# A block of adaLN, sliding-window attention and token MLP: four token groups in a pipeline instead of three stages one after another

## The chip, the cores and the metric

The kernel runs on one core of a Trainium2 chip. The metric is the device time of one execution in microseconds. A core has five engines that run their own instruction streams and wait for each other by semaphores: TensorE (PE, with its weight loads shown as PEld), VectorE (DVE), ScalarE (ACT), GpSimd (POOL) and SyncE (SP), which here issues DMAs. Matmul results land in PSUM, everything else lives in SBUF.

## The reference

x is 2048 tokens of width 512; there are 32 heads of width 16, a window of 256 tokens, and a token MLP whose hidden size is 1792.

```python
mod = (silu(c) @ w_mod).reshape(1, 6, 1, -1)          # sa, ca, ga, sb, cb, gb
h = layernorm(x) * (1 + ca) + sa
x = x + ga * attention(h, wqkv, wo)
h = layernorm(x) * (1 + cb) + sb
x = x + gb * token_mlp(h, w1, b1, w2, b2)

def attention(x, wqkv, wo):                            # H = 32, Dh = 16, W = 256
    q, k, v = split(x @ wqkv)
    scores = q @ k.T * Dh ** -0.5
    mask = (i - j >= 0) & (i - j < W)
    return softmax(where(mask, scores, -1e9)) @ v @ wo

def token_mlp(x, w1, b1, w2, b2):                      # mixes tokens, not channels
    u = gelu(einsum('bsd,sf->bdf', layernorm(x), w1) + b1)
    return (einsum('bdf,fs->bds', u, w2) + b2).transpose(0, 2, 1)
```

## The kernel before

The tokens are 16 blocks of 128 (`tb`, `kb`). The work stands in three stages. A planner orders the instructions of each engine by priority and readiness, so program order is only a hint.

**Stage 1 (lines 182 to 253).** For four groups of four blocks: LN1 on DVE with the square root on ACT (L192 to L202), transposes on PE (L207), scale and shift on ACT into `h1T` (L211), V for the group (L221, evacuated by ACT at L226 or DVE at L231), and Q and K of the first eight heads (L161, L168). K is written twice, once with the odd heads' rows set to zero and once with the even ones' (L172 to L177), so that scores can contract over 32 rows. The modulation vectors come from `w_mod` by small matmuls (L124) and broadcast ones (L245). Pool writes the constant part of the V tile, 16 memsets of 128x512 (L148), and the identity and masks.

**Stage 2, attention (L305 to L374).** Eight passes `hs` of four heads (one of two parities of a set of eight heads), each over 16 key blocks `kb`: 128 steps. A step multiplies one key block with the up to three query blocks that see it: scores (L289, contraction over 32 rows, up to 12 matmuls of 128 columns for four heads in two PSUM tiles `pss`), two exponentials of up to 768 columns on ACT (L317), the mask on DVE, which multiplies the diagonal and the far block in place (L329, L334), and PV (L347): for each head up to three matmuls with 32 stationary columns, 16 of V and 16 of ones, so that the row sums come with the product. Every fourth step DVE evacuates, transposes and divides (L357 to L374). The projections of the later heads are drawn in every fourth step up to step 44 (`pending_proj`, L255 and L324).

**Stage 3.** For each block (L424 to L473): Wo and the residual (L429, L433), LN2, modulation, the MLP's own LN, into `hb`, while the first six of 14 columns of B1 collect (L398). Then the other eight in pairs (L499) with GELU built from ACT and DVE steps (L405 to L420), and y = w2 x GELU (L519) in four groups of four blocks, each followed by two DVE steps and a store (L526 to L532). w1 and w2 are read when attention is over.

Of the kernel before, what the change touches and what calls it, by code (L numbers as in the profile page):

```python
# [8 lines left out]
DT = mybir.dt  # L9
ACT = mybir.ActivationFunctionType  # L10
ALU = mybir.AluOpType

# [5 lines left out]
WIN = 256  # L18
# [3 lines left out]
NF = F // P  # L22
EPS = 1e-5
SCORE_SCALE = DH ** -0.5
GELU_C0 = 0.044715
GELU_C1 = 1.5957691216057308


@with_exitstack
def kernel(  # L30
# [15 lines left out]
    assert tuple(A_x.shape) == (1, S, D)  # L46
    assert tuple(A_wqkv.shape) == (D, 3 * D)
    assert tuple(A_wo.shape) == (D, D)
    assert tuple(B_w1.shape) == (S, F)
    assert tuple(B_w2.shape) == (F, S)  # L50
    assert tuple(c.shape) == (1, D)
    assert tuple(w_mod.shape) == (D, 6 * D)

    x_dram = A_x[0]
    out_dram = out[0]
    dma = nc.sync

    const = ctx.enter_context(tc.tile_pool(name="const", bufs=1))
    small = ctx.enter_context(tc.tile_pool(name="small", bufs=4))
    xpool = tc.alloc_tile_pool(name="xpool", bufs=1)  # L60
    xres = [xpool.tile([P, D], DT.bfloat16, name=f"x{t}") for t in range(NT)]
# [7 lines left out]
    ident_v = identity[:].rearrange("p (a two d) -> p a two d", two=2, d=DH)  # L69
    mask_even = const.tile([P, 1], DT.float32, name="mask_even")  # L70
    nc.vector.tensor_reduce(
        out=mask_even[:], in_=ident_v[:, :, 0, :], axis=mybir.AxisListType.XY, op=ALU.add,
    )
    mask_odd = const.tile([P, 1], DT.float32, name="mask_odd")
    nc.vector.tensor_reduce(
        out=mask_odd[:], in_=ident_v[:, :, 1, :], axis=mybir.AxisListType.XY, op=ALU.add,
    )

    modFM = const.tile([P, 8], DT.float32, name="modFM")
    bc_ga = const.tile([P, D], DT.bfloat16, name="bc_ga")  # L80
    bc_cb1 = const.tile([P, D], DT.bfloat16, name="bc_cb1")
    bc_sb = const.tile([P, D], DT.bfloat16, name="bc_sb")
    bc_gb = const.tile([P, D], DT.bfloat16, name="bc_gb")
# [3 lines left out]
    modw = tc.alloc_tile_pool(name="modw", bufs=1, side="right")  # L87
    with tc.tile_pool(name="modps", bufs=2, space=bass.MemoryType.PSUM) as modps:
        wmod = modw.tile([P, ND, 6 * D], DT.bfloat16, name="wmod")
        w_mod_v = w_mod.rearrange("(j p) n -> p j n", p=P)  # L90
        c4 = modw.tile([ND, P], DT.bfloat16, name="c4")
        dma.dma_start(out=c4[:], in_=c.rearrange("o (j p) -> (o j) p", p=P))
        for t in range(4):
            dma.dma_start(out=xres[t][:], in_=x_dram[t * P : (t + 1) * P, :])
        for v in (0, 1):
            dma.dma_start(out=wmod[:, :, v * D : (v + 1) * D], in_=w_mod_v[:, :, v * D : (v + 1) * D])
        for t in range(4, 8):
            dma.dma_start(out=xres[t][:], in_=x_dram[t * P : (t + 1) * P, :])
        wqkv = const.tile([P, ND, 3 * D], DT.bfloat16, name="wqkv")
        wqkv_v = A_wqkv.rearrange("(j p) n -> p j n", p=P)  # L100
        for j in range(ND):
            dma.dma_start(out=wqkv[:, j, :], in_=wqkv_v[:, j, :])
        for t in range(8, NT):
            dma.dma_start(out=xres[t][:], in_=x_dram[t * P : (t + 1) * P, :])
        for v in (2, 4, 3, 5):
            dma.dma_start(out=wmod[:, :, v * D : (v + 1) * D], in_=w_mod_v[:, :, v * D : (v + 1) * D])

        sig4 = modw.tile([ND, P], DT.float32, name="sig4")
        nc.scalar.activation(out=sig4[:], in_=c4[:], func=ACT.Sigmoid)
        silu4 = modw.tile([ND, P], DT.bfloat16, name="silu4")  # L110
        nc.vector.tensor_tensor(out=silu4[:], in0=c4[:], in1=sig4[:], op=ALU.mult)
        st_ps = modps.tile([P, ND], DT.bfloat16, name="st_ps")
        nc.tensor.transpose(st_ps[:], silu4[:], identity[0:ND, 0:ND])
        sT = modw.tile([P, ND], DT.bfloat16, name="sT")
        nc.vector.tensor_copy(out=sT[:], in_=st_ps[:])
        sT_rep = modw.tile([P, ND, P], DT.bfloat16, name="sT_rep")
        nc.vector.tensor_copy(out=sT_rep[:], in_=sT[:].unsqueeze(2).to_broadcast([P, ND, P]))

        ps_fm = modps.tile([P, 8], DT.float32, name="ps_fm")
        for v in range(2):  # L120
            for oc in range(ND):
                col = v * ND + oc
                for k in range(ND):
                    nc.tensor.matmul(  # L124
                        ps_fm[:, col : col + 1],
                        lhsT=wmod[:, k, v * D + oc * P : v * D + (oc + 1) * P],
                        rhs=sT[:, k : k + 1],
                        start=(k == 0), stop=(k == ND - 1),
                    )
        nc.vector.tensor_copy(out=modFM[:, 0:4], in_=ps_fm[:, 0:4])  # L130
        nc.vector.tensor_scalar_add(out=modFM[:, 4:8], in0=ps_fm[:, 4:8], scalar1=1.0)

        b1b = modw.tile([P, NF], DT.bfloat16, name="b1b")
        dma.dma_start(out=b1b[:], in_=B_b1.rearrange("(j p) -> p j", p=P))
        nc.vector.tensor_copy(out=b1FM[:], in_=b1b[:])
        b2b = modw.tile([P, NT], DT.bfloat16, name="b2b")
        dma.dma_start(out=b2b[:], in_=B_b2.rearrange("(j p) -> p j", p=P))
        nc.vector.tensor_copy(out=b2FM[:], in_=b2b[:])

    otpool = tc.alloc_tile_pool(name="otpool", bufs=1)  # L140
    OTd = [otpool.tile([P, S], DT.bfloat16, name=f"OTd{g}") for g in range(ND)]
    kvpool = tc.alloc_tile_pool(name="kvpool", bufs=1)
    QT = [kvpool.tile([P, S], DT.bfloat16, name=f"QT{g}") for g in range(ND)]
    KeT = [kvpool.tile([P, S], DT.bfloat16, name=f"KeT{g}") for g in range(ND)]
    KoT = [kvpool.tile([P, S], DT.bfloat16, name=f"KoT{g}") for g in range(ND)]
    VaugT = kvpool.tile([P, NT, H, 2 * DH], DT.bfloat16, name="VaugT")
    for t in range(NT):
        nc.gpsimd.memset(VaugT[:, t, :, DH : 2 * DH], 1.0)  # L148

    def vaug_lhsT(t, head):  # L150
        return VaugT[:, t, head, :]

    pj = tc.alloc_tile_pool(name="pj", bufs=1)
    h1T = pj.tile([P, ND, S], DT.bfloat16, name="h1T")
    ps_big = tc.alloc_tile_pool(name="ps_big", bufs=2, space=bass.MemoryType.PSUM, side="right")

    def emit_qk_proj(g8, tg, evac_act):
        tok = slice(tg * 4 * P, (tg + 1) * 4 * P)
        pq = ps_big.tile([P, 4 * P], DT.float32, name="psb")
        for dc in range(ND):  # L160
            nc.tensor.matmul(  # L161
                pq[:], lhsT=wqkv[:, dc, g8 * P : (g8 + 1) * P], rhs=h1T[:, dc, tok],
                start=(dc == 0), stop=(dc == ND - 1),
            )
# [398 lines left out]
```

## Time and profile before

| | us |
|---|---|
| median of 3 runs | 411.39 (407.42 to 419.1) |
| span of the profiled execution | 404.0 |
| busy in it: PE, DVE, ACT, POOL | 350.6, 279.5, 267.8, 8.7 |

The span runs from the first to the last instruction; the launch around it is in the runs' times and not in the span. A row of the slices gives 40 equal parts of the span, each digit the busy share in tenths; PEclk is the clock that TensorE was granted, in tenths of full speed. A matmul's end is modelled and matmuls overlap, so a busy PE need not be PE at its limit: the distance from one start to the next says more than a duration.

### The profile page before, as it was taken

What the parts mean: (1) busy time and instruction counts of PE and PEld (TensorE: products, weight loads), DVE (VectorE), ACT (ScalarE), POOL (GpSimd) and SP (SyncE); (2) the same over time, 40 slices, a digit from 0 to 9 for tenths busy, and PEclk for the clock granted to TensorE, in tenths of its full rate; (3) what the DMA queues carried; (4) which work ended last, traced back from release to release, by engine and by line L of the source; (5) the groups of instructions that cost most, each with busy time, mean ns of one, the idle gap of its engine ahead of it and who ended that gap; (6) DMA issues with size and microseconds to landing.
All of it is one profiled execution on the core that took longest, in us unless ns stands there. A gap on an engine that the chain in (4) does not pass through costs nothing.

```text
span 404.0 us, 8898 instructions
## 1 busy us (share of the span) xinstructions
PE 350.6 (87%) x3713; PEld 168.9 (42%) x3713; DVE 279.5 (69%) x656; ACT 267.8 (66%) x426; POOL 8.7 (2%) x24
## 2 busy tenths in 40 slices
PE   0898997999998898988889988998996799899993
PEld 0543443444444444544444444533342344344441
DVE  6795676688978587757687666679996597522344
ACT  3486588788988888978788878859997554300000
POOL 8000000000000000000000000000000000000000
PEclk9999999699999655555555555569999999999997
DMA  7970000000000000000000000007900592001111
GB/s 221 357 152 0 2 2 2 2 2 2 2 2 2 3 2 2 2 2 2 2 2 2 2 2 2 2 2 287 408 34 0 205 412 112 0 6 48 53 54 53
DMA packets 17169, 24.70 MB, mean 61 GB/s; under 512 B 5096, under 2 KB 12776, under 8 KB 17128
## 3 DMA queue, kind: packets, MB, share of 16 engines
q1 hardware_dynamic: 17128, 24.13, 17.0%
q8 instruction: 29, 0.48, 0.5%
q14 instruction: 12, 0.10, 0.1%
HBM read 22.03 MB, written 2.10 MB: 60 GB/s over the span
## 4 chain that ended last, share of the span: by engine, by line
PE 55%; DVE 21%; ACT 18%; issue 5%; DMA 1%; SPq 0%; ACTq 0%; DVEq 0%
PE pss L289 13%; PE psb L347 13%; ACT et L317 12%; PE py L519 12%; PE pu L499 7%; PE psb L161 3%; DVE ln_stats L455 2%; PE psb L168 2%; DVE ln_stats L436 2%; PE psb L221 2%; DVE et L329 2%; ACT h1T L211 2%; DVE ln_stats L192 1%; PE psb L429 1%; ACT gelu_a L405 1%
## 5 line engine op out<-in xcount | busy, mean ns | idle before, releaser
L317 ACT ACTIVATE et<-pss 128x768 bf16<-128x768 f32 (+2 forms) x256 | 179.5, 779 | 30.4 <-PE psb L347 27.9
L329 DVE TENSOR_TENSOR et<-et,mask_661 128x1024 bf16<-128x1024 bf16 x112 | 75.3, 678 | 25.5 <-ACT et L317 25.0
L347 PE MATMUL psb<-et,VaugT 128*32 128x128 bf16 x1440 | 78.4, 276 | 1.8 <-DVE et L329 0.7
L347 PEld LDWEIGHTS <-VaugT 128*32 128x32 bf16 x1440 | 37.6, 110 | 40.4 <-issue 34.4
L519 PEld LDWEIGHTS <-w2r 128*128 128x128 bf16 x224 | 21.9, 98 | 28.0 <-issue 1.8
L161 PE MATMUL psb<-h1T,wqkv 128*128 128x512 bf16 x64 | 21.5, 398 | 1.2 <-DVE t_1654 L357 0.4
L168 PE MATMUL psb<-h1T,wqkv 128*128 128x512 bf16 x64 | 18.4, 384 | 1.9 <-DVE t_1101 L357 0.4
L499 PEld LDWEIGHTS <-w1r 128*128 128x128 bf16 x128 | 12.5, 98 | 16.6 <-issue 1.2
L221 PE MATMUL psb<-wqkv,h1T 128*128 128x512 bf16 x64 | 17.6, 401 | 1.9 <-ACT QT_196 L165 0.8
L289 PE MATMUL pss<-QT_198,KoT_206 32*128 32x128 bf16 x180 | 16.0, 297 | 3.1 <-ACT et L317 2.9
L289 PE MATMUL pss<-QT_199,KeT_203 32*128 32x128 bf16 x180 | 16.0, 296 | 2.7 <-ACT et L317 2.7
L289 PE MATMUL pss<-QT_198,KeT_202 32*128 32x128 bf16 x180 | 16.0, 296 | 2.7 <-ACT et L317 2.7
L289 PE MATMUL pss<-QT_199,KoT_207 32*128 32x128 bf16 x180 | 16.3, 297 | 2.4 <-ACT et L317 2.2
L289 PE MATMUL pss<-QT_197,KoT_205 32*128 32x128 bf16 x180 | 15.3, 286 | 3.2 <-ACT et L317 3.0
L398 PEld LDWEIGHTS <-w1r 128*128 128x128 bf16 x96 | 9.7, 101 | 19.7 <-issue 10.8
L417 ACT ACTIVATE gelu_sg<-gelu_inner 128x512 bf16<-128x512 bf16 x14 | 8.8, 630 | 11.9 <-DVE gelu_inner L413 11.9
L409 DVE SCALAR_TENSOR_TENSOR gelu_sq<-gelu_a 128x512 bf16<-128x512 bf16 x14 | 9.6, 687 | 7.3 <-ACT gelu_a L405 7.1
L289 PE MATMUL pss<-QT_196,KeT_200 32*128 32x128 bf16 x180 | 11.4, 220 | 3.2 <-ACT et L317 2.4
L289 PE MATMUL pss<-QT_196,KoT_204 32*128 32x128 bf16 x180 | 11.9, 228 | 0.4 <-ACT et L317 0.4
L289 PEld LDWEIGHTS <-KoT_207 32*128 32x128 bf16 x180 | 7.6, 115 | 10.6 <-issue 10.3
L289 PE MATMUL pss<-QT_197,KeT_201 32*128 32x128 bf16 x180 | 11.3, 217 | 0.5 <-ACT et L317 0.2
L289 PEld LDWEIGHTS <-KoT_206 32*128 32x128 bf16 x180 | 7.5, 115 | 9.9 <-issue 9.7
(523 smaller groups left out, 570.0 us busy)
## 6 DMA issues: line engine op xcount, KB each, us to landing
w1r<-in_B_w_dram SPq DMA_DIRECT2D x16, 448.0 KB, 9.0
w2r<-in_B_w_dram SPq DMA_DIRECT2D x14, 512.0 KB, 9.5
wmod<-in_w_mod_dram SPq DMA_DIRECT2D x6, 512.0 KB, 6.1
out_dram<-otile SPq DMA_DIRECT2D x16, 128.0 KB, 1.7
wqkv<-in_A_wqkv_dram SPq DMA_DIRECT2D x4, 384.0 KB, 6.2
wod<-in_A_wo_dram SPq DMA_DIRECT2D x4, 128.0 KB, 3.4
x_64<-in_A_x_dram SPq DMA_DIRECT2D x1, 128.0 KB, 2.1
x_65<-in_A_x_dram SPq DMA_DIRECT2D x1, 128.0 KB, 2.2
```

The source lines that it names most:

```text
L161: nc.tensor.matmul(pq[:], lhsT=wqkv[:, dc, g8 * P : (g8 + 1) * P], rhs=h1T[:, dc, tok], start=(dc == 0), stop=(dc == ND - 1),)
L168: nc.tensor.matmul(pk[:], lhsT=wqkv[:, dc, D + g8 * P : D + (g8 + 1) * P], rhs=h1T[:, dc, tok], start=(dc == 0), stop=(dc == ND - 1),)
L221: nc.tensor.matmul(pv[:], lhsT=h1T[:, dc, tb * P : (tb + 1) * P], rhs=wqkv[:, dc, 2 * D : 3 * D], start=(dc == 0), stop=(dc == ND - 1),)
L289: nc.tensor.matmul(pss[:, jj, r * P : (r + 1) * P], lhsT=Ksel[rows, kb * P : (kb + 1) * P], rhs=qt[rows, qb * P : (qb + 1) * P], start=Tru ...
L317: nc.scalar.activation(out=et[:, 2 * a : 2 * a + 2, 0:nr, :], in_=cur[a][:, :, 0 : nr * P].rearrange("p h (r q) -> p h r q", q=P), func=AC ...
L329: nc.vector.tensor_tensor(out=et[:, :, 0:3:2, :], in0=et[:, :, 0:3:2, :], in1=mask01[:].unsqueeze(1).to_broadcast([P, 4, 2, P]), op=ALU.mult,)
L347: nc.tensor.matmul(po[32 * j : 32 * j + 32, qi, :], lhsT=vaug_lhsT(kk, head), rhs=ering[kk][:, j, r, :], start=(idx == 0), stop=(idx == le ...
L398: nc.tensor.matmul(pu[:, i, :], lhsT=w1r[:, sc, fc * P : (fc + 1) * P], rhs=hb[sc][:], start=(sc == 0), stop=(sc == NT - 1),)
L409: nc.vector.scalar_tensor_tensor(out=sq[:], in0=a[:], scalar=GELU_C0, in1=a[:], op0=ALU.mult, op1=ALU.mult,)
L417: nc.scalar.activation(out=sg[:], in_=inner[:], func=ACT.Sigmoid, scale=GELU_C1)
L499: nc.tensor.matmul(pu[:, i, :], lhsT=w1r[:, sc, fc * P : (fc + 1) * P], rhs=hb[sc][:], start=(sc == 0), stop=(sc == NT - 1),)
L519: nc.tensor.matmul(py[:, tl, :], lhsT=w2r[:, fc, tb * P : (tb + 1) * P], rhs=guT[fc][:], start=(fc == 0), stop=(fc == NF - 1),)
```

## The change

The kernel is written in a fixed program order for each engine (`manual_schedule`), over four token groups of four blocks. Attention is 192 steps, 48 for each group `g`: for each set of eight heads `g8` (4), parity `par` (2), pair of heads `a` (2), three steps `t`, whose scores fill two PSUM banks each (one for each head). Six steps, one parity of four heads, are called a quad here. Scores contract over 16 rows; the odd heads' Q and K are copies that a DMA moves up by 16 rows. Each exponential covers 1024 columns, except that the third step of group 0 has 256. The scores of step k+2 are issued behind the exponential of step k; there are two score tiles.

The mask is now two `affine_select` on Pool for each pair of heads (8 blocks of 128 each). PV runs one quad behind, in steps 2 to 5 of the next quad. V is padded with zeros in 64-column pieces so that both parities add into one PSUM tile `pa`; the row sums come from matmuls of their own with a tile of ones, into `pb`. One division of the sums serves a whole group.

Between the steps stand fillers. In group 0's first 14 steps: V, the Q and K of its later heads, and the modulation broadcasts. In each group: LN1 of the next group, its transposes, its Q, K and V in halves of two matmuls, and, one group late, division, Wo, LN2 and the MLP's LN of the last group. The last group's are in a tail, with B1 rounds of the first four columns between. LN uses `Ln` and `Exp` on ACT in place of the square root. Half of w1 is loaded in group 0, the other half and w2 behind the attention. B1 runs in groups of 4, 4, 4 and 2 columns; the residual and b2 go into x ahead of y, and y is evacuated by one addition.

```diff
+WINDOWS = [(0, 0, 3, 0), (1, 1, 3, 3), (2, 2, 2, 6), (3, 3, 1, 9), (-1, 0, 2, 10), (-2, 0, 1, 8)]
+BANKS = [
+    [(0, 0, 3, 0), (1, 1, 1, 3)],
+    [(1, 2, 2, 0), (2, 2, 2, 2)],
+    [(-2, 0, 1, 0), (3, 3, 1, 1), (-1, 0, 2, 2)],
+]
...
+    ctx.enter_context(tc.manual_schedule())
...
+    misc = tc.alloc_tile_pool(name="misc", bufs=2, space=PSUM)
+    ps_ab = tc.alloc_tile_pool(name="ps_ab", bufs=1, space=PSUM)
+    ps_sc = tc.alloc_tile_pool(name="ps_sc", bufs=2, space=PSUM, side="right")
...
+    Vz = [att.tile([P, GT, H // 2, 64], DT.bfloat16, name=f"Vz{r}") for r in range(3)]
+    for r in range(3):
+        for tl in range(GT):
+            nc.gpsimd.memset(Vz[r][:, tl], 0.0)
...
+    def rstd(mv, name):
+        nc.scalar.activation(out=lv[:], in_=mv[:, :, 1], func=ACT.Ln, bias=eps_t[:], scale=1.0)
+        nc.scalar.activation(out=rs[:], in_=lv[:], func=ACT.Exp, scale=-0.5)
...
+    def qk_half(g, g8, which, half, on_act=False):
+        for dc in (0, 1) if half == 0 else (2, 3):
+            nc.tensor.matmul(
+                ps[:], lhsT=wqkv[:, dc, col : col + P], rhs=h1T[g][:, dc, :],
+                start=(dc == 0), stop=(dc == ND - 1),
+            )
...
+            nc.vector.tensor_copy(out=ev[:], in_=ps[:])
+        nc.sync.dma_start(out=od[0 : P - DH, :], in_=ev[DH:P, :])
...
+    def rec_piece(g, i):
+            nc.vector.reciprocal(out=rec[g][:, i * P : (i + 1) * P], in_=bsb[g][:, i * P : (i + 1) * P])
...
+    def norm_out(g, g8):
+        nc.tensor.matmul(ps[:], lhsT=sel[:, g8, :], rhs=rec[g][:], start=True, stop=True)
+        nc.vector.tensor_tensor(out=OT[(g, g8)][:], in0=Asb[(g, g8)][:], in1=ps[:], op=ALU.mult)
...
+    def ln2_h(g, tl):
+        normed(h, xg[g][:, tl, :], mv2[g], rs2[g], tl)
+        nc.vector.tensor_tensor(out=h, in0=h, in1=bc[4][:], op=ALU.mult)
+        nc.vector.tensor_tensor(out=h, in0=h, in1=bc[3][:], op=ALU.add)
+        ln_stats(h, mv3[g][:, tl, :])
...
+        if g == 0:
+            for tl in range(GT):
+                for half in (0, 1):
+                    at(tl, v_half, 0, tl, half)
+            u = 4
+            for g8 in (1, 2, 3):
+                for which in (0, 1):
+                    for half in (0, 1):
+                        at(u, qk_half, 0, g8, which, half)
+                    u += 1
+            at(10, mod_bc, 2)
...
+            at(16, wo_scale)
+            at(17, load_w1a)
+            ln, tt, qkv0 = 6, 19, 24
+        else:
+            ln, tt, qkv0 = 0, 12, 24
...
+    def post(at, g, u):
+        for i in range(4):
+            at(u + i, rec_piece, g, i)
+        for g8 in range(ND):
+            at(u + 5 + g8, norm_out, g, g8)
+        for tl in range(GT):
+            for half in (0, 1):
+                at(u + 10 + 2 * tl + half, wo_half, g, tl, half)
+            at(u + 12 + 2 * tl, ln2_stats, g, tl)
+        at(u + 23, ln2_rstd, g)
+        for tl in range(GT):
+            at(u + 24 + 2 * tl, ln2_h, g, tl)
+        at(u + 36, ln3_rstd, g)
+        for tl in range(GT):
+            at(u + 37 + tl, ln3_hb, g, tl)
...
+        diag = ef[:, 0:24:3, :]
+        nc.gpsimd.affine_select(
+            out=diag, in_=diag, pattern=[[0, 8], [1, P]],
+            compare_op=ALU.is_ge, fill=0.0, base=0, channel_multiplier=-1,
+        )
+        far = [ef[:, 2:24:3, :]] if g else [e[:, :, 2, :], e[:, :, 5, :]]
...
+        for j in range(4):
+            nc.tensor.matmul(
+                pa[(g, g8)][32 * j : 32 * j + 32, cols],
+                lhsT=vt[:, m % GT, 4 * g8 + j, 32 * par : 32 * par + 32], rhs=rhs,
...
+        for j in range(4):
+            nc.tensor.matmul(
+                pb[g][32 * j : 32 * j + 32, cols],
+                lhsT=ones8[:, 7 - i : 39 - i], rhs=rhs,
...
+    for k, (g, g8, par, a, t) in enumerate(steps):
+        u = k % 48
+        if u == 0:
+            todo = fillers(g)
+        emit_exp(k)
+        if k + 2 < len(steps):
+            emit_scores(k + 2)
+        s = k % 6
+        if s >= 2 and k >= 6:
+            q = steps[k - 6][:3]
+            for wi in pv_share(q, s):
+                emit_pv(q, wi)
+        for fn in todo.pop(u, []):
+            fn()
...
+    fgroups = [list(range(0, 4)), list(range(4, 8)), list(range(8, 12)), [12, 13]]
...
+    post(lambda u, fn, *a: tail.setdefault(u, []).append(lambda: fn(*a)), NG - 1, 0)
...
+    first = [ps_m1.tile([P, D], DT.float32, name=f"pu{4 + i}") for i in range(4)]
+    for fc in range(NF):
+        for tb in range(4):
+            y_mm(first[tb][:], fc, tb)
...
-                if nr == 3:
-                    nc.vector.tensor_tensor(
-                        out=et[:, :, 0:3:2, :], in0=et[:, :, 0:3:2, :],
-                        in1=mask01[:].unsqueeze(1).to_broadcast([P, 4, 2, P]), op=ALU.mult,
-                    )
```

More of the change, by code (lines that the diff above doesn't have):

```diff
@@ L67 @@
     nc.vector.memset(eps_t[:], EPS)
[L69 to L72, printed above, removed]
-    )
[L74 to L77, printed above, removed]
+    ones8 = const.tile([P, 40], DT.bfloat16, name="ones8")
@@ L147, with bank @@
[L147 to L160, printed above, removed]
+    def bank(dtype=DT.float32):
+        return misc.tile([P, D], dtype, name="mz")
```

781 lines of the change are left out of this document (391 added, 390 removed).

## The prediction

> **What bounds the kernel now.** I read the slices first, then busy time by stage, the waits, the forms of the exponential, and last the order in which TensorE starts its matmuls.
>
> ```profile
> span 404.0 us, 8898 instructions
> PE   0898997999998898988889988998996799899993
> ACT  3486588788988888978788878859997554300000
> PEclk9999999699999655555555555569999999999997
> ```
>
> ```profile
> 46.80:133.50 86.70, 78.34 (x1197) 38.13 (x1196) 66.86 (x136) 73.59 (x112) 0.00 (x0) 0.96 0.01 2
> 133.50:267.70 134.20, 120.23 (x1771) 61.96 (x1770) 93.06 (x170) 111.02 (x160) 0.00 (x0) 0.50 0.01 2
> 267.70:313.00 45.30, 38.50 (x181) 16.03 (x174) 40.40 (x160) 38.02 (x80) 0.00 (x0) 0.95 0.43 163
> ```
>
> The columns are busy us on PE, PE's loads, DVE, ACT and POOL, then the granted clock. Attention fills 46.8 to 267.7, 221 us; TensorE's clock falls to 0.50 there once the Q/K projections are used up, yet the steps keep their pace.
>
> ```profile
> ACT et L317 <- PE psb L347: 27.9, 58, 1.3
> PE pss L289 <- ACT et L317: 16.5, 52, 0.5
> ```
>
> ```profile
> L317 ACT ACTIVATE et<-pss 128x768 bf16<-128x768 f32 x224 | 165.7, 820 | 23.1 <-PE psb L347 20.6 <-PE pss L289 1.2
> L317 ACT ACTIVATE et<-pss 128x512 bf16<-128x512 f32 x16 | 8.7, 595 | 3.3 <-PE psb L347 3.3
> L317 ACT ACTIVATE et<-pss 128x256 bf16<-128x256 f32 x16 | 5.3, 385 | 4.1 <-PE psb L347 4.1
> L329 DVE TENSOR_TENSOR et<-et,mask_661 128x1024 bf16<-128x1024 bf16 x112 | 75.3, 678 | 25.5 <-ACT et L317 25.0
> ```
>
> So attention is a loop: two exponentials, the DVE mask, PV, the next scores. ACT is busy 184.6 of 220.9 us and waits the rest for it. Before it stand 46.8 us of LN1 and V; behind it 45 us of Wo and LN2.
>
> **The change, part by part.** It removes the mask from DVE and from the loop (Pool masks a whole quad that PV reads a quad later), and spreads QKV and Wo over the steps. 192 steps replace 128, with 48 for each of four token groups and six to a quad.
>
> *Exponentials.* Busy by count is 0.33, 0.54 and 0.74 us for 256, 512 and 768 columns, 0.20 to 0.21 for each 256, so 0.94 for 1024. 176 of these and 16 of 256 make 171 us: 5.64 us a quad, 35.4 in group 0.
>
> *TensorE.* Starts with the clock full:
>
> ```profile
> 111.52 0.36 PE L347 MATMUL psb<-et,VaugT 128*32 128x128 bf16 x12
> 111.82 0.39 PE L168 MATMUL psb<-h1T,wqkv 128*128 128x512 bf16 x1
> 112.14 0.36 PE L347 MATMUL psb<-et,VaugT 128*32 128x128 bf16 x10
> ...
> 112.97 0.35 PE L289 MATMUL pss<-QT_197,KeT_201 32*128 32x128 bf16 x6
> 113.25 0.39 PE L168 MATMUL psb<-h1T,wqkv 128*128 128x512 bf16 x1
> ```
>
> and at half clock:
>
> ```profile
> 200.03 0.51 PE L289 MATMUL pss<-QT_198,KoT_206 32*128 32x128 bf16 x6
> 200.47 0.62 PE L347 MATMUL psb<-et,VaugT 128*32 128x128 bf16 x12
> ```
>
> and the 224 matmuls of y, whose first and last groups are:
>
> ```profile
> L519 PE MATMUL py<-guT_4835,w2r x16: 376/379/379, 348.5 to 385.4; 128*128 128x512 bf16 x16
> L519 PE MATMUL py<-guT_4848,w2r x16: 379/379/379, 359.7 to 396.6; 128*128 128x512 bf16 x16
> ```
>
> A full matmul is (396.6 - 348.5)/223 = 0.216 us, 0.054 for 128 columns. Twelve PV matmuls side by side in fours are 3 x 0.054 = 0.16, and took 0.30; six scores in pairs are also 0.16, and took 0.28; a full one followed by PV took 0.32. So 0.10 to 0.14 is left whenever the shape of the tiles changes; I take 0.11 (half clock: 0.44 - 0.32 = 0.12, I take 0.13). The new code alternates the row or column tiles, so pairs and fours should hold. A quad then streams scores 6 x 512 x 0.42 ns = 1.28 us and PV 12 blocks x 0.054 x 2 = 1.28, because the row sums now have matmuls of their own. Without filler there are 8 changes: 3.4 us, below ACT's 5.64. With a filler half of two full matmuls in each step: 2.59 more and 16 changes, 1.28 + 1.28 + 2.59 + 1.76 = **6.91 us, over ACT: TensorE becomes the bound there**, 1.15 a step.
>
> Group 0: steps 0 to 13 carry four full matmuls each, 0.86 + scores 0.16 + two changes 0.22 = 1.24 (1.59 in the four with PV), 18.8; 2 for a clock not yet up; ten light steps 7.4; 24 filled ones at 9 blocks, 4 x 6.27 = 25.1: 53.3. Groups 1 and 2: steps 0 to 10 at 0.94, 11 to 15 at 1.0, 32 at 1.15: 52.2 each. Group 3 has no next QKV: 10.3 + 4.7 + 9.2 + 22.6 = 46.8. Attention: **204.5**.
>
> *Clock.*
>
> ```profile
> 70.00:80.00 10.00, 9.65 (x121) 3.97 (x118) 6.41 (x14) 7.12 (x13) 0.00 (x0) 0.66 0.01 2
> ```
>
> Streaming on the whole array is about 24% of the 0.96 stage (the code puts 12 projection pairs there: 12 x 8 x 0.216 = 20.7 of 86.7 us), plus PV's 0.16 of each 1.7 us step: 33% in all; in the 0.50 stage it is PV's 10% alone. Filled stretches have (2.59 + 1.28)/6.91 = 56%: full. Light ones have 1.28/5.64 = 23%, between the two; I take half. Then a light quad is 2 x 2.56 + 8 x 0.13 = 6.2, over ACT by 0.56, on 57 light steps 5.3. The one short dip lasted (1 - 0.66)/0.5 x 10 = 6.8 us; if half of that is the way back, each of four returns runs 3.4 us at 12.4 a quad (2 x 5.15 + 16 x 0.13) instead of 6.9 and loses 1.5. **+10**, bounded by 0 and, at half clock everywhere, +110 (rival 3).
>
> [...]
>
> *Pool.*
>
> ```profile
> 1.74 7.05 POOL L148 MEMSET VaugT<- 128x512 bf16 x15
> 8.74 0.33 POOL L260 TENSOR_SCALAR_AFFINE_SELECT mask_661<-mask_661 128x128 bf16<-128x128 bf16 x1
> 9.04 0.29 POOL L264 TENSOR_SCALAR_AFFINE_SELECT mask_661<-mask_661 128x128 bf16<-128x128 bf16 x1
> ```
>
> Two selects of 1024 elements come every three steps (2.82 us); only 128-element ones exist, 0.30 from start to start. Upper end 8 x 0.30 = 2.4 us; lower 0.30 + 896 elements at the memset's 0.47/512 = 1.1. I take 1.1, the longer row: 2.2 of 2.82 is hidden. PV comes to its mask 2.8 us after the last exponential, so it doesn't wait; if it did, the next scores stand behind it on TensorE, and ACT behind those. Past 1.41 Pool paces the light quads.
>
> *DVE.*
>
> ```profile
> 6.06 0.29 DVE L194 BATCH_NORM_AGGREGATE ln_mv<-ln_stats 128x2 f32<-128x6 f32 x2
> 6.43 2.50 DVE L202 TENSOR_SCALAR xn_247<-x_64,ln_mv,ln_rstd 128x512 bf16<-128x512 bf16 x1
> 9.04 0.42 DVE L202 TENSOR_SCALAR xn_261<-x_65,ln_mv,ln_rstd 128x512 bf16<-128x512 bf16 x1
> ```
>
> ```profile
> L231 DVE CAST VaugT<-psb 128x512 bf16<-128x512 f32 x8 | 5.5, 685 | 4.2 <-PE psb L221 4.2
> L200 DVE RECIPROCAL ln_rstd<-ln_sd 128x1 f32<-128x1 f32 x16 | 2.3, 152 | 2.3 <-ACT ln_sd L196 2.2
> L362 DVE RECIPROCAL zr<-t_817 x1: 243/243/243, 57.5 to 57.5; 128x16 f32<-128x16 bf16 x1
> 290.75 0.42 DVE L452 TENSOR_TENSOR h_5148<-xn_5146,bc_cb_93 128x512 bf16<-128x512 bf16 x1
> 291.63 0.69 DVE L436 BATCH_NORM_STATS2 ln_stats<-x_10_4806 128x6 f32<-128x512 bf16 x1
> 292.24 0.68 DVE L455 BATCH_NORM_STATS2 ln_stats<-h_5148 128x6 f32<-128x512 bf16 x1
> ```
>
> A group needs 12 statistics of 0.61 + 0.15, 12 normalizations of 0.35, 8 products or sums of 0.42, 29 reads of PSUM of 0.65, and 4 reciprocals of 0.152 + 127 x 0.0061 = 0.92: 40 us of 52. Covered on average; steps 6 to 15 hold 11 us in 9.4, up to 2 us a group, left to the range. The odd heads' copies by DMA on SP have some six steps before they are read: nothing. On SP they pass the first half of w1, which waits there for the modulation weights to be done with (step 14); group 1 reads its copies 20 steps after that. The two rstd instructions of a LayerNorm on ACT lie in filled steps, under TensorE, or cost some tenths in light ones.
>
> *Start.*
>
> ```profile
> 46.85 3.01 ACT L317 ACTIVATE et<-pss 128x768 bf16<-128x768 f32 x4
> 15.41 2.72 PE L221 MATMUL psb<-wqkv,h1T 128*128 128x512 bf16 x7
> ```
>
> xn_247 ended at 8.93, just after Pool's memsets. The new ones are 12 of 1024, 12 x 0.94 = 11.3 from about 1.8, so normalization starts near 13; four of 0.35, two small copies, four h1T of 0.65, then Q and K at 0.39 a cold matmul (3.1) with two evacuations and the first scores: **21** instead of 46.85.
>
> *After the last exponential.* Two selects 2.3, PV 1.6, evacuations 1.3, reciprocals 3.7, norm_out 3.0, Wo with statistics 6.1, the two rstd 0.9 each, h2 4 x 1.95 = 7.8, hb and the last B1 2.4: **30**. Twelve of the sixteen B1 rounds lie under it, as does w1b.
>
> *MLP.*
>
> ```profile
> L409 DVE SCALAR_TENSOR_TENSOR gelu_sq<-gelu_a 128x512 bf16<-128x512 bf16 x14 | 9.6, 687 | 7.3 <-ACT gelu_a L405 7.1
> L417 ACT ACTIVATE gelu_sg<-gelu_inner 128x512 bf16<-128x512 bf16 x14 | 8.8, 630 | 11.9 <-DVE gelu_inner L413 11.9
> 400.91 0.43 DVE L531 TENSOR_TENSOR otile<-o_6127,x_15_4811 128x512 bf16<-128x512 bf16 x1 [0.16 <-DMA out_dram<-otile]
> ```
>
> 160 matmuls of B1 34.5, 224 of y 48.4. In program order each GELU runs gelu_a, two DVE steps, gelu_sg before the next gelu_a: 0.65 + 1.3 + 0.63 = 2.6. The last group has only 32 matmuls (6.9 us) over four GELUs and a fifth gelu_a that frees y's first bank (11.4): a bubble of **4.5**. **87.4**. One addition and the last store, 3.1 from 400.91 to the end of the span: **3**.
>
> Sum: 21 + 204.5 + 30 + 87.4 + 3 = 346; with the clock 356. The profiled span, 404.0, lies 7.4 under the median of 411.39; I add that: **363 us**.
>
> **Rivals.**
> 1. *The clock holds* in light stretches: 346 + 7 = 353.
> 2. *ACT paces everything* (changes of shape overlap): filled quads at 5.64 and group 0's first steps at about 1.0 make attention 176 to 180: 325. For: those 0.11 are leftovers of starts; against: every one of the three kinds shows it.
> 3. *Slower: the clock stays at half.* The same counts at half clock give groups of 87, 84.5, 84.5 and 58: attention 314, time 463. It decides once 10 of some 16 filled quads run so (5.5 each, 57 to pass 420). For: 134 us of 0.50 before; against: 56% streaming.
> 4. *Pool is slower than 1.41.* Pool paces every quad at 4T (3T in group 0): 120T, at 2.0 us 240 against 214, 390. Past 2.26 the kernel is slower.
> 5. *Pool blocks DVE.* xn_247 took 2.50 instead of 0.42 while Pool wrote. If 20 such instructions a group wait 0.8 (Pool busy 0.76 of the time, half of 2.2), DVE has 56 us a group and binds: about +4 in each of three groups, 375. Against: xn_261 lost nothing beside a select. [...]
>
> **Numbers.** Forecast 46% (own range 348 to 380), clock holds 14%, ACT paces 12%, Pool blocks DVE 10%, Pool slow 10% (half under 403, half within 2%), slower 8%. Range 325 to 402, which leaves out half of 4 and all of 3. Faster by over 2% 0.87, within 2% 0.05 (about what a measurement of this kernel can tell from no change), slower 0.08.
>
> **What would show it.** First exponential near 21; TensorE, not ACT, without gaps in the filled stretches and steps of 1.15 there; PEclk falling early in groups 1 to 3 and at the end of 3; selects near 1.1 us; 30 us from the last exponential to full matmul rate; a gap of 4 to 5 us ahead of y. Selects over 1.4, or PEclk at half in filled stretches, make it wrong.

## The result, and the profile after

| | before | after |
|---|---|---|
| median of all runs, us | 409.74 (407.42 to 419.1, 4 runs) | 427.45 (426.42 to 432.09, 4 runs) |
| span of the profiled execution | 404.0 | 424.8 |

The changed kernel is slower: 1.0483 times before, interval 1.04 to 1.0566. The forecast was 363 us and faster; slower had a chance of 0.08, and the range ended at 402. Ratios here and below leave out runs disturbed by over 1.5%; medians and ranges are of all runs.

The slices of the changed kernel, in the same form as before:

```profile
span 424.8 us, 7343 instructions
PE   0699899999999989999798998987918999299996
ACT  1256666885455897568556765882003343300000
PEclk9989579855555985569655556558977999689999
```

TensorE is busy as forecast, ACT is not the bound. But PEclk is at 5 or 6 in 17 of the 26 slices of attention (2 to 27). By stage (columns as before: busy us of PE, PE's loads, DVE, ACT, POOL, then the clock):

```profile
21.00:75.00 54.00, 51.93 (x448) 16.17 (x452) 26.73 (x49) 34.61 (x47) 27.75 (x44) 0.85 0.37 115
75.00:130.00 55.00, 52.11 (x469) 15.77 (x474) 27.41 (x48) 35.23 (x40) 23.93 (x26) 0.56 0.02 5
130.00:185.00 55.00, 51.02 (x551) 17.57 (x557) 37.61 (x65) 39.34 (x44) 28.27 (x26) 0.69 0.05 14
185.00:240.00 55.00, 49.79 (x499) 15.34 (x506) 30.00 (x50) 36.14 (x41) 26.09 (x24) 0.66 0.06 18
240.00:280.00 40.00, 36.56 (x382) 11.89 (x382) 19.26 (x35) 28.47 (x31) 19.93 (x19) 0.54 0.01 1
```

The first exponential starts at 19.3, the last ends at 289.3: attention takes 270 us where the sum had 204.5. Half clock lasts from 81.9 for 54.6 us, from 157.0 for 30.7, from 204.8 for 58.0 and from 266.3 for 23.9; with two shorter ones, from 20.5 for 3.4 and from 44.4 for 13.7, that is 184 of the 270 us. What that does to a quad with filler is seen at the exponentials that open one; first two that lie a quad apart with the clock full, then two at half:

```profile
194.18 2.05 ACT L442 ACTIVATE et<-sc 128x1024 bf16<-128x1024 f32 x2
...
201.12 1.02 ACT L442 ACTIVATE et<-sc 128x1024 bf16<-128x1024 f32 x1 [0.55 <-PE sc L425]
```

```profile
112.92 1.02 ACT L442 ACTIVATE et<-sc 128x1024 bf16<-128x1024 f32 x1 [1.73 <-PE sc L425]
...
125.00 1.02 ACT L442 ACTIVATE et<-sc 128x1024 bf16<-128x1024 f32 x1 [1.31 <-PE sc L425]
```

6.94 and 12.08 us a quad: the prices of the sum (6.91 and 12.4) hold. Wrong is how many quads pay the second: nine take 10.3 to 12.3 us. The waits and the groups of the page:

```profile
ACT et L442 <- PE sc L425: 84.1, 112, 2.1
PE pu L539 <- DVE hb L148: 10.4, 1, 10.4
PE pu L626 <- ACT gelu_a L577: 9.1, 2, 4.8
```

```profile
L442 ACT ACTIVATE et<-sc 128x1024 bf16<-128x1024 f32 x176 | 175.0, 1023 | 85.0 <-PE sc L425 84.1
L450 POOL TENSOR_SCALAR_AFFINE_SELECT et<-et 128x1024 bf16<-128x1024 bf16 x64 | 71.4, 1115 | 145.1 <-ACT et L442 109.4
```

ACT now waits 84.1 us for scores. Behind attention, TensorE waits 10.4 us for the last group's `hb`, and 9.1 ahead of y; the clock falls to half in each of these waits and comes back behind it (314.0 to 324.2 and 365.2 to 375.5).

One of the starts of half clock, 204.8, lies in the middle of a stretch with filler, behind a wait. The timeline there:

```profile
200.92 1.19 DVE L253 TENSOR_TENSOR h<-h,bc 128x512 bf16<-128x512 bf16 x1
...
201.79 1.27 POOL L456 TENSOR_SCALAR_AFFINE_SELECT et<-et 128x1024 bf16<-128x1024 bf16 x1
...
202.15 1.19 DVE L254 TENSOR_TENSOR h<-h,bc 128x512 bf16<-128x512 bf16 x1
...
202.48 0.60 PE L177 MATMUL mz<-h1T,wqkv 128*128 128x512 bf16 x2
...
204.20 0.67 DVE L189 CAST QTe<-mz 128x512 bf16<-128x512 f32 x1
...
204.93 1.01 PE L177 MATMUL mz<-h1T,wqkv 128*128 128x512 bf16 x2 [1.52 <-DVE QTe L189]
```

LN2's product and sum (L253, L254) take 1.19 us beside a select, not 0.43; the read of PSUM (L189) stands behind them on DVE, TensorE waits 1.52 us for its bank, its longest wait in attention, and its next two matmuls already run at half (1.01 us for the pair, 0.60 at 202.48).

### The profile page after: what moved, and what is told of

Its sections match the earlier page's. It is cut to its first block, busy times and chain, and to the rows that moved or that the text cites. A ratio compares the mean times of both kernels' runs of the same rounds, so it can differ in the third digit from the quotient of the medians.

```text
span 424.8 us, 7343 instructions
## 1 busy us (share of the span) xinstructions
PE 366.1 (86%) x3035; PEld 132.9 (31%) x3075; DVE 231.1 (54%) x416; ACT 205.7 (48%) x248; POOL 145.7 (34%) x164
## 4 chain that ended last, share of the span: by engine, by line
PE 74%; DVE 13%; ACT 8%; issue 3%; DMA 1%; POOL 0%; POOLq 0%; SPq 0%; ACTq 0%; DVEq 0%
PE sc L425 17%; PE pu L626 12%; PE pu L539 9%; PE pa L481 9%; PE mz L177 7%; PE pb L489 6%; ACT et L442 6%; PE mz L231 5%; PE mz L199 5%; DVE st L127 2%; PE mz L159 2%; DVE h L254 1%; PE mz L221 1%; DVE h L253 1%; DMA xg<-in_A_x_dram 1%
## 5 line engine op out<-in xcount | busy, mean ns | idle before, releaser
L442 ACT ACTIVATE et<-sc 128x1024 bf16<-128x1024 f32 x176 | 175.0, 1023 | 85.0 <-PE sc L425 84.1
L450 POOL TENSOR_SCALAR_AFFINE_SELECT et<-et 128x1024 bf16<-128x1024 bf16 x64 | 71.4, 1115 | 145.1 <-ACT et L442 109.4
L481 PE MATMUL pa<-et,Vz 128*32 128x384 bf16 (+2 forms) x704 | 64.7, 362 | 1.2 <-POOL et L456 1.2
L456 POOL TENSOR_SCALAR_AFFINE_SELECT et<-et 128x1024 bf16<-128x1024 bf16 (+1 forms) x80 | 65.6, 830 | 0.0
L489 PE MATMUL pb<-et,ones 128*32 128x384 bf16 (+2 forms) x704 | 63.7, 371 | 0.0
L626 PE MATMUL pu<-guT,w2r 128*128 128x512 bf16 x219 | 51.1, 393 | 9.6 <-ACT gelu_a L577 9.1
L425 PE MATMUL sc<-QTo,KTo 16*128 16x256 bf16 (+2 forms) x416 | 49.2, 338 | 6.7 <-ACT et L442 5.0
L425 PE MATMUL sc<-QTe,KTe 16*128 16x256 bf16 (+2 forms) x416 | 45.6, 321 | 7.9 <-ACT et L442 5.1
L177 PE MATMUL mz<-h1T,wqkv 128*128 128x512 bf16 x113 | 41.5, 454 | 3.3 <-DVE QTe L189 1.5
L539 PE MATMUL pu<-hb,w1a 128*128 128x512 bf16 x109 | 29.8, 399 | 10.5 <-DVE hb L148 10.4
L497 DVE CAST Asb<-pa 128x512 bf16<-128x512 f32 x16 | 11.1, 691 | 39.5 <-PE pa L481 39.5
L622 DVE TENSOR_TENSOR otile<-pu,xg 128x512 bf16<-128x512 f32 x16 | 10.8, 690 | 36.0 <-PE pu L626 33.7
L539 PE MATMUL pu<-hb,w1b 128*128 128x512 bf16 x110 | 26.7, 379 | 0.1
L237 DVE TENSOR_TENSOR xg<-mz,xg 128x512 bf16<-128x512 f32 x16 | 11.1, 692 | 22.8 <-PE mz L231 22.6
```

The lines of the kernel that those rows point to most:

```text
L177: nc.tensor.matmul(ps[:], lhsT=wqkv[:, dc, col : col + P], rhs=h1T[g][:, dc, :], start=(dc == 0), stop=(dc == ND - 1),)
L425: nc.tensor.matmul(ps[:, jj, col * P : (col + nq) * P], lhsT=kt[rows, kc : kc + P], rhs=QT[(g, g8)][par][rows, q0 * P : (q0 + nq) * P], st ...
L442: nc.scalar.activation(out=e[:, :, 4 * t : 4 * t + 4, :], in_=ps[:].rearrange("p h (r q) -> p h r q", q=P), func=ACT.Exp, scale=SCORE_SCALE,)
L450: nc.gpsimd.affine_select(out=diag, in_=diag, pattern=[[0, 8], [1, P]], compare_op=ALU.is_ge, fill=0.0, base=0, channel_multiplier=-1,)
L456: nc.gpsimd.affine_select(out=blocks, in_=blocks, pattern=[[0, 8 if g else 2], [-1, P]], compare_op=ALU.is_ge, fill=0.0, base=-1, channel_ ...
L481: nc.tensor.matmul(pa[(g, g8)][32 * j : 32 * j + 32, cols], lhsT=vt[:, m % GT, 4 * g8 + j, 32 * par : 32 * par + 32], rhs=rhs, start=(par ...
```

## The experiments

Theories. **C**: light steps stream too little on the whole array, the clock halves there, and a filled stretch at half clock doesn't win it back soon. **B**: Pool's selects hold DVE up, TensorE falls idle, and the clock halves. **W**: the pipeline is simply more work for TensorE, and the clock is a side effect.

**Full and thin dummies.** One matmul that nothing reads goes ahead of the scores in 82 light steps, those with no or few full matmuls as filler.

```diff
+    def light(k):
+        g, u = k // 48, k % 48
+        return 14 <= u < 24 if g == 0 else u < 16 or (g == 3 and u >= 24)
...
+        if light(k):
+            nc.tensor.matmul(ps[:, 0, :], lhsT=wqkv[:, 0, 0:P], rhs=wqkv[:, 1, 0:D], start=True, stop=True)
```

The second kernel has the same with 16 contraction rows (`wqkv[64 * a : 64 * a + DH, ...]`): the same columns to stream, an eighth of the array's rows.

> Adds one matmul of full size (128 rows, 128 columns, 512 wide) to each of the 82 light steps, into the score tile that the scores then overwrite; the output is the same. Clock theory (the loss is TensorE at half clock in the filled quads, which follow light steps in which it falls): the clock stays up, filled quads take 6.9 us instead of 12.1, attention 270 falls to 220-235 us, the time from 427 to 375-395. Work theory (TensorE has too much to do and too many changes of shape at any clock): 82 x (0.22 to 0.43 + a change of 0.11) = 27 to 45 us more, 455-470. Pool theory (selects hold up DVE, DVE holds up TensorE): no gain, 427 or a few us more.

> The same 82 extra matmuls, but contracting over 16 rows instead of 128, so that they stream as long and use an eighth of the array; output the same. If the clock follows how long TensorE streams: like the full ones, 375-395. If it follows how much of the array works: the clock falls as before, 427 plus 82 x 0.2 to 0.4, 440-460. Work theory: 440-460 too, but then the full ones as well.

Full: 401.91 us (387.94 to 417.5, 4 runs), ratio to before 0.9437 [0.9284, 0.959]. Thin: 449.53 (447.49 to 463.36), ratio 1.0868 [1.075, 1.0985]. Two stages of each, the full one first:

```profile
75.00:130.00 55.00, 50.60 (x610) 17.54 (x609) 40.98 (x70) 42.98 (x47) 31.82 (x31) 0.93 0.06 16
130.00:185.00 55.00, 53.55 (x641) 18.58 (x640) 34.71 (x61) 43.12 (x50) 29.74 (x28) 0.89 0.04 12
```

```profile
130.00:185.00 55.00, 51.32 (x447) 16.53 (x450) 31.20 (x55) 31.69 (x36) 23.78 (x22) 0.56 0.05 14
240.00:280.00 40.00, 38.19 (x325) 11.98 (x317) 14.40 (x23) 23.03 (x24) 16.34 (x16) 0.50 0.00 1
```

W falls: 82 more matmuls made the kernel 25 us faster by the medians, whose runs scatter by 30 us; the median lies above the 375 to 395 expected. In the profiled run with full dummies a drop of 20.5 us begins in a stretch with filler (122.0), and the light steps begin none but one of 6.8 at the end of attention (251.7). With the thin ones TensorE is busy 38 of 40 us and the clock stays at 0.50, so being busy did not hold it here; that points to how much of the array streams. (Some thin dummies run beside the scores on other rows, both starting at 39.91, so they add less streaming time too; these two runs don't part rows and time; a count over the traces of before and after does, see below.) By the prediction's count the light quads hold 1.28 us of full streaming in 5.64 (23%); six dummies of 0.216 make that 46%.

**No mask.** The selects on Pool are left out, so the softmax is unmasked.

```diff
-        nc.gpsimd.affine_select(out=diag, ...)
-            nc.gpsimd.affine_select(out=blocks, ...)
```

> Leaves out the Pool selects, so that the softmax isn't masked. Pool theory: DVE's two-input operations go from up to 1.3 us back to 0.42, the stalls of TensorE on evacuations (1.5 us at 205 us) go, the clock isn't lost in the middle of filled stretches: 427 falls by 15 to 40 us. Clock theory alone: the light steps lose the clock as before, within 5 us of 427. Work theory: within 5 us.

398.91 us (395.34 to 403.35), ratio 0.9573 [0.9437, 0.9708]. LN2's product, in the changed kernel and then without the mask (minimum, median and maximum in ns):

```profile
L253 DVE TENSOR_TENSOR h<-h,bc x16: 424/426/1227, 129.5 to 317.6; 128x512 bf16<-128x512 bf16 x16
```

```profile
L253 DVE TENSOR_TENSOR h<-h,bc x16: 424/426/426, 125.7 to 287.0; 128x512 bf16<-128x512 bf16 x16
```

No product is held up any more, and the 58 us that began in the stretch with filler are gone. Four drops of some length remain in attention, all beginning in light steps (81.2 for 41.0, 149.5 for 20.5, 207.5 for 20.5, 238.2 for 23.9). So B and C are both real, and here of like size: each alone gives back 25 to 29 us by the medians, 31 to 38 by the shortest runs.

**GELU in another order.** `gelu_a` of a whole group first, y's first banks from the other pool, part of the residual behind the last GELU.

```diff
+        for fc in fgroups[gi - 1]:
+            emit_gelu_a(fc)
         for fc in fgroups[gi - 1]:
             emit_gelu(fc)
```

> Issues the GELU inputs of a group ahead of its GELU steps, and gives y the PSUM banks that are free first; the output is the same. All theories: attention unchanged, the 9 us that TensorE waits ahead of y shrink to 1 to 2 us and the half clock behind them goes: 427 falls by 8 to 13 us.

417.65 us (407.32 to 423.27, 10 runs), some 10 us less than the changed kernel; against before not to be told from it, 1.0068 [0.9954, 1.0182]. The 9.1 us ahead of y and the half clock behind them go, as expected.

**Spread fillers.** V of a group in its own first eight steps, one half a step, in place of the group before; Q and K halves in two of every three steps.

```diff
+            for tl in range(GT):
+                for half in (0, 1):
+                    at(2 * tl + half, v_half, g, tl, half)
...
+                        u += 1
+                    u += 1
```

> Moves V of a group from the last eight steps of the group before into its own first eight, and spaces the Q and K halves two in three steps over steps 24 to 47; nothing is added, the output is the same. Clock theory: the first eight steps keep the clock, so steps 16 to 47 start at full clock more often; 427 falls to 395-415, less than with the extra matmuls since steps 8 to 15 stay thin. Work theory: same work, within 5 us of 427. Pool theory: fewer evacuations meet the LN2 operations, a few us less at most.

423.26 us (404.17 to 424.14, 4 runs), 4 us under the changed kernel, too little to tell apart; the 395 to 415 expected did not come. Drops of 37.5 us from 51.0, 20.5 from 167.0 and 51.2 from 208.0 remain among others. My reading, which this run does not isolate: a thinner filler gives fewer light steps but also less with which to win the clock back.

**Both at once, and the LN2 half split.** First: the dummies, and no mask. Then, with the mask and the dummies, LN2's second half in three parts over three steps. Third: dummies, spread fillers, GELU order and the split together.

```diff
-            at(u + 24 + 2 * tl, ln2_h, g, tl)
+            for part in range(3):
+                at(u + 24 + 3 * tl + part, ln2_h, g, tl, part)
```

> Both at once: the extra full matmul in the 82 light steps, and no Pool selects (the softmax isn't masked). If thin steps and DVE held up by Pool are together the whole loss in attention, no filled quad is left at half clock: attention 210-220 us instead of 270, 233 and 239, the time 370-380. If a third cause is left, some filled quads still take 10 to 12 us and the time stays above 385.

> The extra full matmuls, selects kept, and the four DVE operations of LN2's modulated input, which stood in one step for each block, spread over three steps each; output the same. Pool theory: a held-up operation no longer has two more and a statistic behind it ahead of the evacuation, the stalls ahead of a half-filled bank shrink, and the half clock near 122 us goes: 402 falls to 375-388 and its runs lie closer together. If the mere presence of the selects costs (not the burst): no change from 402.

> Together: V and Q/K spread, GELU inputs first, LN2's operations split, the extra full matmul only where no real one is left (steps 14 to 23 of group 0, 8 to 15 of the others, the last 24); output the same. By the clock and Pool theories attention comes to 205-215 us and the MLP to about 90, the time to 350-365, under the 411 of before. By the work theory 415-425.

381.54 us (373.92 to 392.29), 0.9251 [0.9175, 0.9327]; 392.61 (391.62 to 404.55), 0.9665 [0.9621, 0.971]; 379.33 (375.22 to 379.78), 0.9324 [0.9255, 0.9393]. All three medians lie above what was expected (370 to 380, 375 to 388, 350 to 365). The longest run of the first is the profiled one: half clock from 85.1 for 51.2 us, begun in light steps of group 1 that have their dummy, so one dummy did not hold the clock there. The second still has a drop of 30.7 us from 85.9 there. In the second and third, quads at the turn of a group have become slow (12.8 to 13.1 us, then 10.8 and 11.1 in the third): ACT waits there some 4 us for LN2's statistics, which the split had made later.

**The turn of a group.** The split in two parts; then also 36 dummies in the tail where TensorE waits for `hb`; and the split in two alone on the changed kernel.

```diff
-            for part in range(3):
-                at(u + 24 + 3 * tl + part, ln2_h, g, tl, part)
+            for part in range(2):
+                at(u + 24 + 2 * tl + part, ln2_h, g, tl, part)
...
+    keep = misc.tile([P, D], DT.float32, name="mz")
+    for _ in range(36):
+        nc.tensor.matmul(keep[:], lhsT=wqkv[:, 0, 0:P], rhs=wqkv[:, 1, 0:D], start=True, stop=True)
```

> e8_spread_all with LN2's second half in two parts instead of three (normalization and product in one step, sum and statistics in the next), so that the last statistics are done by step 38 of a group and the rstd on ACT in step 42 finds them. Clock theory: in e8_spread_all the last quads of groups 1 and 2 (12.8 us) and the first of groups 2 and 3 (10.8, 11.1) are slow because ACT waited 4 us for those statistics, TensorE fell idle and the clock halved; without that wait they go back to 5.9 and some 6.2, 23 us less: about 356 us, with no half clock in attention. Rival, the light steps with one dummy lose the clock by themselves at the turn of a group: no change, 379.

> e9_h_two with 36 full matmuls (7.8 us at 0.216) that nothing reads, placed behind the twelfth B1 round of the first group, where TensorE stands idle for 7.8 us and then runs 5.5 us of B1 at half clock. Clock theory: the clock stays full there, 5.5 us of work at half become 2.75: some 3 us less than e9_h_two, provided that the idle time is no shorter than 7.8. If the work itself counts (they delay what follows): 0 to 3 us more.

> The changed kernel with nothing but LN2's second half in two parts (no dummies, mask left on Pool). Theory that a bunch of DVE operations held up by Pool's selects in one step starts the drops inside filled stretches: half as many held operations stand ahead of a PSUM read, the drops that begin at 204.8 and the like vanish, those from light steps stay: 395 to 412 us, near the run without the mask (399). Rival, what counts is the sum of held operations in a group: no change, 427.

e9_h_two: 385.37 us (370.54 to 392.92, 6 runs), 0.9164 [0.9056, 0.9273]; not the 356 expected. Its timeline shows why, first ACT, then DVE, then TensorE:

```profile
122.14 0.30 ACT L132 ACTIVATE r_lv<-mv,eps_t 128x4 f32<-128x4 f32 x1 [3.25 <-DVE mv L128]
```

```profile
115.25 1.19 DVE L254 TENSOR_TENSOR h<-h,bc 128x512 bf16<-128x512 bf16 x1
116.47 1.19 DVE L256 TENSOR_TENSOR h<-h,bc 128x512 bf16<-128x512 bf16 x1
...
121.92 0.18 DVE L128 BATCH_NORM_AGGREGATE mv<-st 128x2 f32<-128x6 f32 x1
```

```profile
123.64 0.61 PE L436 MATMUL sc<-QTo,KTo 16*128 16x384 bf16 x4 [2.17 <-ACT et L453]
```

Even with its work put earlier DVE is late: held at 1.19 us an operation it falls behind, step after step, and ACT's wait of 3.25 us comes with it. The reading of e8_spread_all (the split made it late) was too small.

e10_tail_fill: 377.68 (368.61 to 389.98, 6 runs), 0.9094 [0.9009, 0.9179]. From 271.7 us on, 5 us behind the last exponential, the clock is full up to the end of y, where e9_h_two had 0.50 for 10.2 us from 283.9; its shortest run is 1.9 us under that of e9_h_two, the expected sign, and the scatter of attention covers the size. e11_h_two_only: 408.04 (401.43 to 416.49, 11 runs), 0.9872 [0.9782, 0.9963]: the drop from 204.8 is gone, those of the light steps stay (54.6, 30.7, 30.7 and 27.3 us). As expected under B.

**Both causes taken apart.** The MLP's LN of groups 0 and 1 moves into the next group (on e10_tail_fill); then the same without the dummies of the light steps, without the mask, and with two dummies a step. Beside them e9_h_two without most of the row sums (e12).

```diff
-        at(u + 36, ln3_rstd, g)
-        for tl in range(GT):
-            at(u + 37 + tl, ln3_hb, g, tl)
+        if g not in (0, 1):
+            ln3(at, g, u + 36)
...
+        if g > 1:
+            ln3(at, g - 2, 3)
```

> e10_tail_fill with the MLP's LN of groups 0 and 1 (rstd on ACT in step 42, four normalizations behind it) moved nine steps on, into steps 3 to 7 of the group after. In e9_h_two DVE was still behind at step 42, with sums and products of 1.19 instead of 0.43 us, and ACT waited 3.25 us for the last statistics. Clock theory: without that wait TensorE doesn't fall idle at the turn of a group, the clock stays full: the last quads of groups 1 and 2 go from 12.0 to 5.9, the first of groups 2 and 3 from 10.8 to 6.2, 21 us less than the shorter runs of e10_tail_fill (369): 346 to 356 us, with less scatter. Rival, the light steps lose the clock at the turn in any case: 365 to 390 as before.

> e13_late_ln3 without the dummies in the light steps, and nothing else. If light steps lose the clock by their small share of full streaming, half clock comes back in the stretches that had dummies and lasts on into the filled ones: 25 to 55 us more than e13_late_ln3. If the stalls behind DVE were the whole cause, the dummies are only work: the same as e13_late_ln3 or up to 5 us less.

> e13_late_ln3 without Pool's selects, so the softmax is unmasked, and nothing else. In e13_late_ln3 TensorE still waits 1.25 us twice for PSUM reads (QTe) that stand behind DVE operations of 1.19 us, and half clock begins behind such places. If DVE held up by Pool is what is left, every operation is back at 0.42, no half clock is left in attention, and it takes some 210 us as the prediction's sum without the clock had it (204.5): 348 to 358 us in all. If light steps still lose the clock by themselves: 365 or more.

> e13_late_ln3 with two dummies (0.43 us of full streaming) in each light step instead of one, 82 more. If one dummy a step is still too small a share in the steps without PV (half clock began at 142.6 in a light stretch), that drop goes: 360 to 368 us. If the stalls behind DVE are what is left, the dummies only add 82 x 0.216 = 18 us at most, where ACT doesn't cover them: 377 to 395.

> e9_h_two with the row sums' own matmuls left out for all but the first quad of a group (so the divisor is not the softmax sum; the ones tile is all ones). That is half of PV's streaming. Plain work: a filled quad loses 0.64 us (12 blocks x 0.054), 6.9 to 6.3, some 16 of them and part of the tail: 10 us less than e9_h_two. Clock theory: PV's matmuls use the whole array, so a quad's share of full streaming falls too (0.64 of 1.28 us gone); in steps with one dummy it goes from about 45% towards 33%, and the clock may be lost there: then 10 to 40 us more instead.

| run | median, us | runs |
|---|---|---|
| e13_late_ln3 | 377.39 | 6, 369.75 to 379.38 |
| e14_late_no_dummy | 403.79 | 6, 386.65 to 432.21 |
| e15_late_no_mask | 352.05 | 4, 347.38 to 353.62 |
| e16_late_two_dummies | 374.0 | 4, 369.89 to 377.32 |
| e12_no_sums | 382.27 | 4, 370.86 to 395.71 |

e13 came out at 377 and not at the 346 to 356 expected: the later LN alone doesn't keep the clock. The ranges of e13, e14 and e15 don't touch. From e13 to e14, the dummies away: 26 us more, and the last stage of attention is all at half clock. From e13 to e15, the selects away: 25 us less. The last stage of attention in e14_late_no_dummy, and two in e15_late_no_mask with its slices:

```profile
207.00:277.00 70.00, 64.86 (x628) 20.00 (x634) 33.84 (x58) 47.85 (x53) 32.68 (x31) 0.50 0.01 3
```

```profile
span 348.9 us, 7269 instructions
PEclk9989999999999999999999999988999999999999
```

```profile
75.00:130.00 55.00, 53.51 (x727) 20.22 (x736) 40.28 (x79) 50.60 (x59) 0.00 (x0) 1.00 0.07 19
130.00:185.00 55.00, 52.95 (x728) 20.52 (x734) 38.28 (x76) 49.76 (x57) 0.00 (x0) 1.00 0.07 19
```

With neither cause left, the clock stays full from 25.1 us to 226.4, when the last exponential starts, attention takes 207.8 us, and every quad from the third of group 0 on takes 5.3 to 8.4. What e13_late_ln3 still had (377 us) went with the selects. Twice TensorE waits there 1.25 us for QTe behind held operations, and half clock begins at 122.1 and 187.0; the first of these waits:

```profile
119.74 0.59 PE L177 MATMUL mz<-h1T,wqkv 128*128 128x512 bf16 x2 [1.25 <-DVE QTe L189]
```

Its third drop, 142.6, begins in light steps, where TensorE waits 2.15 us for the reciprocals of the division on DVE. Two dummies a step (e16) end that one and cost about as much as they save: 374 us lies in neither expected range, and can't be told from e13's time. e12_no_sums, run beside e9_h_two, settles nothing: the two scatter over the same range, and 10 us of plain work can't be seen in it.

Of the kernels that compute everything, e16_late_two_dummies has the lowest median (374.0 us, ratio to before 0.9114 [0.9039, 0.9189]); e8_spread_all, e10_tail_fill and e13_late_ln3 are not told apart from it. All beat both the kernel before and the changed one.

## Why the prediction was wrong

| part, us | sum | after | e15_late_no_mask |
|---|---|---|---|
| to the first exponential | 21 | 19.3 | 19.9 |
| attention, without the clock term | 204.5 | 270.0 | 207.8 |
| from the last exponential to the end | 120.4 | 135.5 | 121.2 |
| clock term | 10 | in the rows above | |

*The step that failed* is the clock. The prediction had "Filled stretches have (2.59 + 1.28)/6.91 = 56%: full", and from one short dip a way back of 3.4 us for each of four returns, +10 in all. The runs show two things in its place. First, filled stretches entered at half clock did not come back within 3.4 us: 54.6 us from 81.9 and 30.7 from 157.0 run through light and filled steps alike. The 56% was worked out at full clock; at half clock the same quad takes 12.08 us, and counted at full-clock speed its matmuls are (2.59 + 1.28)/12.08 = 32%, not far above the 23% that lost the clock. Second, the clock was lost inside filled stretches too (at 204.8, for 58.0 us), which the prediction had not priced at all.

A count over the traces of before and after bears the first point out. In their clock records every stretch but the last of each is a whole number of 3.41 us (10.2 is 3 of them, 58.0 is 17). For each such window from 20 us on, count every matmul at its full-clock time (0.216 us for 512 columns), times the part of 128 rows and 128 columns that its form shows, spread over its recorded duration: an estimate of the share of the array that streamed. Of 229 windows, all 115 with a share above 0.39 were followed by a window at full clock, and 99 of the 101 below 0.36 by one at half; 6 of the 115 had half clock themselves, 12 of the 101 the full one. Of the 13 between, 8 were followed by full clock. By this count the 56% lies with those that full clock followed, the 32% with those that half clock followed. The part of the array matters in it: with the matmuls' plain time in place of the share, even the best line puts 52 of the windows on the wrong side, against 5 with the share. The lines were read off traces of this case, and no run was made to test them.

*Pool against DVE* was rival 5, and its mechanism was right: 1.19 us instead of 0.43 is the 0.8 that it assumed. Its price was wrong. It was counted as load on DVE (+4 a group); DVE was busy only 26.7 to 37.6 us of each stage of 54 or 55 from 21 to 240, but at 204.8 a few held operations in a row kept TensorE waiting 1.52 us for a PSUM bank, and 58.0 us of half clock began in that wait. The "against", one normalization that lost nothing beside a select, was too thin. In attention of the changed kernel the seven products and sums that began while a select ran took 1.19 to 1.32 us, the four that had begun before one took 0.42 to 0.43, as did all 16 products without selects (e3_no_mask).

*Rival 3*, half clock with 463 us, had the right price (5.5 us a filled quad by the sum, 5.1 measured) and nearly the right point of decision ("once 10 of some 16 filled quads run so"): nine did, some 46 of the 57 us that it counts, and the tail brought the rest. It got 0.08 because 56% was taken as safe.

*The counts were right, or near.* Filled quads 6.94 (6.91), at half 12.08 (12.4), a light one at half 6.76, from 83.83 to 90.59 (6.2), a select 1.12 (1.1), the first exponential at 19.3 (21); an exponential of 1024 costs 0.99 (0.94). With the clock kept full, e15_late_no_mask gives 19.9 + 207.8 + 121.2 = 348.9 us of span against 346. It has dummies and other orders that the sum has not, and no selects, which the sum holds hidden, so agreement to 1% is in part luck and no test of each term. Of the 79 us by which the changed kernel's span lies above 346, 65 belong to attention; 62 of them are gone in e15_late_no_mask. (The clock term's own parts, 5.3 and 4 x 1.5, make 11.3 and not 10.)

*Tail and MLP* took 15 us more than the sum. The waits ahead of y were 9.1 and not 4.5. The wait for `hb` and the second wait ahead of y each brought 10.2 us of half clock, which a sum of durations at full clock doesn't hold; matmuls ran in 3.8 and 5.6 us of these, so they cost an estimated half of that, some 4.7. The rest isn't broken down. Behind the gaps of 10.4 us and of 4.3 and 4.8 the clock was at half (up to 324.2 and 375.5); in attention the longest gap is the 1.52 us that end at 204.93, and half clock took 184 of the 270 us there all the same.

*Launch*: 7.4 us were added between span and median; the profiled run of the changed kernel took 426.51, 1.7 above its span.

## What to carry over

Price a stretch at both clocks (6.94 and 12.08 us a filled quad here), and ask of each whether it keeps the clock that it has: in the traces of before and after the estimated share of the array that streamed told the clock of the next window in all but 5 of 229, the matmuls' plain time in all but 52. The mask moved to Pool was not free for DVE here, though Pool was busy only 145.7 of 424.8 us: 0.43 us became 1.19. Look at what stands on DVE behind the operations that are held up, a PSUM read above all (1.52 us of waiting on TensorE). A sum can be near in its parts and the time still 79 us off, when one state (the clock) carries a small stall on into the steps that follow.

## What the runs showed of the hardware

- TensorE busy 38 of 40 us was granted 0.50 (16-row dummies, e2_thin_dummy, 240 to 280 us); with full dummies the clock was 0.93 and 0.89 (e1_full_dummy, 75 to 130 and 130 to 185 us).
- In the traces of before and after, from 20 us on, 115 of 115 windows of 3.41 us with an estimated streaming share of the array above 0.39 were followed by full clock, 99 of 101 below 0.36 by half.
- The stretches at half clock that ended within the trace lasted 3.4, 10.2, 13.7, 23.9, 30.7, 54.6 and 58.0 us in the changed kernel, 3.4, 6.8 and 136.5 in the one before. The one of 58.0 began in a wait of 1.52 us.
- In the changed kernel a select of 128x1024 took 1.09 us (the median), beside DVE up to 1.27 and once 2.39; a two-input DVE operation that began in attention while one ran took 1.19 to 1.32 instead of 0.43, and a normalization up to 1.28 instead of 0.41. The four two-input ones in attention that had begun before a select lost nothing (0.42 to 0.43).
